# Raw first-layer weights in 128-partition transfers, queries ahead of keys, and another order of work in the first four chunks

## The chip, the core and the metric

The kernel runs on one core of a Trainium2 chip. The metric is device time in microseconds (us) of one execution; three executions before the change gave 628.51, 629.78 and 630.63, a median of 629.78 us. One execution was taken with the profiler: it took 630.29 us, and its span, from the first to the last profiled instruction, is 628.6 us. All times inside the profile count from the span's start.

## The reference, cut to what matters

A retention layer (linear attention with decay), followed by a two-layer feed-forward block whose activation is h * erf(softplus(h)):

```python
# q, k, v: (4 batches, 8 heads, 768 positions, 64), float32
for t in range(S):
    state = gamma[None, :, None, None] * state + np.einsum('bhd,bhe->bhde', k[:, :, t], v[:, :, t])
    y[:, :, t] = scale * np.einsum('bhd,bhde->bhe', q[:, :, t], state)
x = y.transpose(0, 2, 1, 3).reshape(B * S, H * D)     # 3072 tokens x 512
h = x @ w_in                                          # 512 x 2048
sp = np.maximum(h, 0.0) + np.log1p(np.exp(-np.abs(h)))
g = h * erf(sp)
return (g @ w_out).astype(np.float32)                 # 2048 x 512
```

Both weight matrices are 64-bit floats: `w_in` is 512 x 2048 x 8 bytes, 8.39 MB. The kernel gets them as 64-bit words and makes 32-bit floats of them itself.

## The kernel before, in words

**Tokens.** The 3072 tokens are 24 chunks of 128 (six for each batch). Two chunks make a group of 256 tokens, so there are twelve groups. Within a chunk the retention is two masked matrix products and a product with the running state.

**Weights.** `w_in` is handled in eight raw pieces, n = 0 to 7, each with 256 of the 2048 columns. One raw piece fills a tile `raw` of 128 partitions x 1024 64-bit words (1 MB). Partition p of its lower half (r = 0) holds rows of `w_in` below 256, the upper half (r = 1) those from 256 on, in four blocks g of 64 rows. `load_piece` issues the transfers, on SyncE's queue (SP, line 153). Each transfer before the change writes one half of the partitions: 64 partitions, two or four blocks g, and 128 or 256 columns. `conversion(n)` (lines 184 to 210) turns a raw piece into 32-bit floats: five passes of VectorE (DVE) with one of ScalarE (ACT, line 187) after the first. The pool has four raw tiles; the load of piece n+4 is issued when piece n is converted, and the loads of chunks 4 and 5 stand behind those of pieces 4 and 5.

**Stages.** (1) Four chunks of retention, written out by hand as a list of calls: `T` transposes keys (part 0) or queries (part 1) on TensorE (PE, line 390), `Q_` and `V_` scale queries and values on DVE (line 376), `S_` makes scores (line 402), `M` masks them (line 413), `O_` makes outputs (lines 434, 441, 449), `A` adds to the state (line 459). `keep_warm` puts idle products on PE (line 354). (2) A loop over sixteen column tiles `ft` of 128: `hidden_of(ft, g)` makes the first layer for groups 0 and 1 (line 591); tile ft needs piece ft // 2 converted, and the loop asks for tile ft + 2 ahead. Beside it run the retention of chunks 4 and 5, the loads of chunks 6 and 7 (32-partition transfers, line 123) and the splitting of the weights into high and low parts (lines 247 to 249). `put_hidden` stores each tile (256 KB) through GpSimd's queue (POOL, line 601). (3) Units: groups 2 to 11, eight units each, `unit(g, n)` with all weights on chip (lines 616 and 628), and beside them the rest of the retention and the conversion of `w_out`. (4) Activation and second layer (line 801).

**What sets the order.** Every engine runs its instructions in the order in which the program lists them; nothing reorders them. SP issues its transfers in program order and rotates through eight semaphores, so that a transfer is issued only when the one eight places before it has landed.

The lines that the change touches are `load` (103 to 106), `load_piece` (145 to 158), the opening loads (276 to 283), the guard in `ret_transpose` (393) and the list of calls of stage 1 (649 to 691). A piece is now loaded by

```python
rows = (slice(2), slice(2, 4)) if n == 0 else (slice(4),)
for part, g, r in itertools.product(parts or (None,), rows, range(2)):
```

Of the kernel before, what the change touches and what calls it, by code (L numbers as in the profile page):

```python
# [21 lines left out]
P = 128  # L22
C = 128
JPC = 4
# [17 lines left out]
def kernel(  # L42
# [14 lines left out]
    B, H, S, D = q.shape  # L57
# [5 lines left out]
    n_k = d_model // P  # L63
    n_ft = d_ff // P
    NPC = n_ft // 2
    DH = d_model // 2
# [13 lines left out]
    def b4(name, shape, dtype=F32):  # L80
        return big.tile([P] + shape, dtype, name=name, tag="b4")
# [4 lines left out]
    def b8(name, shape, dtype=F32):  # L86
        return wide.tile([P] + shape, dtype, name=name, tag="b8")
# [5 lines left out]
    KN, QN, V, KB, QB, KT, QT, SC, AM, SU = {}, {}, {}, {}, {}, {}, {}, {}, {}, {}  # L93
    KNP, VP = {}, {}

    def of_chunk(x, j):

        b, c = divmod(j, NC)
        return x[b, :, c * C : (c + 1) * C, :].rearrange("h p d -> p h d")

    def load(j):

        kq = b4("kq", [2, H, D])
        KN[j], QN[j] = kq[:, 0], kq[:, 1]
        for to, src in ((KN[j], k), (QN[j], q)):
            nc.sync.dma_start(to, of_chunk(src, j))  # L106

    def load_values(j):
        if j % 2 == 0:
            VP[j] = b4("v", [2, H, D])  # L110
        V[j] = VP[j - j % 2][:, j % 2]
        nc.sync.dma_start(V[j], of_chunk(v, j))
# [30 lines left out]
    WF, RAW, POWER = {}, {}, {}  # L143
    done = set()

    def load_piece(n, *parts):

        if n not in RAW:
            RAW[n] = b8("raw", [2 * d_model], I64)
        rows = (slice(2), slice(2, 4)) if n == 0 else (slice(4),)  # L150
        for part, g, r in itertools.product(parts or (None,), rows, range(2)):
            f = slice(2 * P) if part is None else slice(part * P, (part + 1) * P)
            nc.sync.dma_start(
                RAW[n][r * D : (r + 1) * D].rearrange("p (g f) -> p g f", g=n_k)[:, g, f],
                w_in[r * DH : (r + 1) * DH, n * 2 * P : (n + 1) * 2 * P].rearrange(
                    "(g p) f -> p g f", p=D
                )[:, g, f],
            )

    def load_quarter(i):  # L160
# [11 lines left out]
    def conversion(n):  # L172
# [5 lines left out]
        for part in range(2) if n < 4 else (None,):  # L178
# [22 lines left out]
            if part != 0:  # L201
                del RAW[n]
                if n + 4 < NPC:
                    load_piece(n + 4)
                if n < 2:
                    load(JPC + n)
                    load_values(JPC + n)
# [13 lines left out]
    def weights():  # L221


        for n in range(2 * NPC):
            yield from conversion(n)

    weight_steps = weights()
# [5 lines left out]
    def need(*what):  # L233
        while what not in done:
            next(weight_steps)
# [34 lines left out]
    nc.scalar.dma_start(d_k, decay_k)  # L270
    nc.scalar.dma_start(d_s, decay_s[::D].rearrange("(o s) h -> o s h", o=1).to_broadcast([P, 2, HP]))
    load(0)

    nc.scalar.copy(idle_out, ident[:, :1])

    for j in range(1, JPC):
        load(j)
        load_values(j - 1)
    load_piece(0, 0)
    load_values(JPC - 1)  # L280
    load_piece(0, 1)
    for n in range(1, 4):
        load_piece(n, 0, 1)

    causal = const.tile([P, C], F32, name="causal")
    nc.gpsimd.memset(causal, 1.0)
# [16 lines left out]
    def query_scale(c):  # L303
        nc.vector.reciprocal(kq_s[:, c, 1], kq_s[:, c, 0])
        nc.vector.tensor_scalar(kq_s[:, c, 1], kq_s[:, c, 1], unscale, None, op0=ALU.mult)
# [14 lines left out]
    def other_scales():  # L320
        query_scale(slice(2, NC))
# [30 lines left out]
    def keep_warm(n):  # L352
        for _ in range(n):
            nc.tensor.matmul(idle, ident, ident, start=True, stop=True)
# [3 lines left out]
    def ret_psum(pool=None):  # L358

        pool = pool or next(psum_turn)  # L360
        return pool.tile([P, HP, C], F32, name="hp" if pool is ps_h else "r")
# [3 lines left out]
    def x_of(j):  # L365

        g, i = divmod(j, 2)
        if i == 0:
            XC[g] = b4("xT", [HP, GT])
        return XC[g][:, :, i * C : (i + 1) * C]  # L370
# [13 lines left out]
    def ret_transpose(j, part=None, names=None):  # L384
        for i, (x, store) in enumerate(((KN[j], KT), (QN[j], QT))):
            if part not in (None, i):
                continue
            p = ps_o.tile([P, HP, C], F32, name=names[i]) if names else ret_psum(ps_h if i else ps_r)
            for u in range(HP):
                nc.tensor.transpose(  # L390
                    p[:, u, :], x[:, 2 * u : 2 * u + 2, :].rearrange("p h d -> p (h d)"), ident
                )
            if i == 0:
                KQT = b4("kqT", [2, HP, C])
                KT[j], QT[j] = KQT[:, 0], KQT[:, 1]
            nc.scalar.copy(store[j], p)
# [20 lines left out]
    def ret_out(j, between=None, state_last=False):  # L417
        c = j % NC
        x = x_of(j)
        pp = [ps_o.tile([P, HP, C], F32, name=f"o{(2 * j + r + 1) % 4}") for r in range(2)]  # L420

        def place(h):
            return pp[h % 2][h // 4 * D : (h // 4 + 1) * D, h % 4 // 2, :]

        if state_last:
            between()


        if c:
            for u in PAIRS:  # L430
                for r in range(2):
                    h = 2 * u + r
                    own = slice(r * D, (r + 1) * D)
                    nc.tensor.matmul(
                        place(h), state[own, u, :], QT[j][own, u, :],
                        start=(h % 4 < 2), stop=False, skip_group_check=True,
                    )
        if between is not None and not state_last:
            between()
        for h in (0, 4, 1, 5, 2, 6, 3, 7):  # L440
            nc.tensor.matmul(
                place(h), V[j][:, h, :], AM[j][:, h % 2, h // 2, :],
                start=(not c and h % 4 < 2), stop=True, skip_group_check=True,
            )

        new = SU[j] = pp[0][:, 2:, :].rearrange("p a (b d) -> p (a b) d", d=D)
        for h in range(H):
            r = h % 2
            nc.tensor.matmul(
                new[r * D : (r + 1) * D, h // 2, :], KN[j][:, h, :], V[j][:, h, :],  # L450
                start=False, stop=True, skip_group_check=True,
            )
        for r in range(2):
            nc.scalar.copy(x[:, r::2], pp[r][:, :2, :])
# [130 lines left out]
    def hidden_of(ft, g):  # L585

        if ft not in HP_:
            HP_[ft] = ps_h.tile([P, 2, GT], F32, name="hp")
        w = WF[ft // 2].rearrange("p h a f -> p (h a) f")
        for kk in range(n_k):  # L590
            nc.tensor.matmul(  # L591
                HP_[ft][:, g],
                w[:, kk, ft % 2 * P : (ft % 2 + 1) * P], XC[g][:, kk],
                start=(kk == 0), stop=(kk == n_k - 1),
            )
# [10 lines left out]
    def unit(g, n):  # L606
# [36 lines left out]

    Q_, V_, T, S_, M, O_, A = (
        scale_q, scale_v, ret_transpose, ret_scores, ret_mask, ret_out, ret_add
    )


    T(0, 0)
    keep_warm(2)  # L650
    Q_(0)
    second_scales()
    T(0, 1)
    keep_warm(1)
    T(1, 0)
    S_(0)
    Q_(1)
    T(1, 1)
    keep_warm(2)
    other_scales()  # L660
    M(0)
    V_(0)
    S_(1)
    Q_(2)
    O_(0)
    T(2, 0)
    M(1)
    A(0)
    T(2, 1)
    V_(1)  # L670
    Q_(3)

    def next_scores():
        S_(2)
        M(2)

    O_(1, next_scores)
    T(3, 0)
    V_(2)
    A(1)  # L680
    T(3, 1)
    need("in", 0)
    O_(2)
    S_(3)
    V_(3)
    next(weight_steps)
    A(2)
    M(3)
    need("in", 1)
    ret_out(JPC - 1, lambda: hidden_of(0, 0), state_last=True)  # L690
    hidden_of(1, 0)


# [217 lines left out]
    for n in range(NG * NU):  # L911
        g, i = divmod(n, NU)
# [62 lines left out]
```

## Time and profile before

| what | value |
|---|---|
| median of three executions | 629.78 us (628.51 to 630.63) |
| profiled execution | 630.29 us, of which span 628.6 us |
| PE busy | 617.5 us, 98% of the span |
| weight loads of PE | 555.9 us, 88% |
| DVE busy | 472.9 us, 75% |
| ACT busy | 346.8 us, 55% |
| POOL busy | 99.8 us, 16% |
| granted clock of TensorE | 0.999 |
| SP's transfers | 67.53 MB, 44.4% of sixteen DMA engines' span |
| POOL's transfers | 37.77 MB, 17.7% |
| raw pieces, 512 KB transfers | 8, median 10.3 us from issue to landing |
| raw pieces, 256 KB transfers | 12, median 6.2 us |
| raw pieces, 128 KB transfers | 8, median 5.5 us |

How to read it: the first rows are busy times of engines over the whole span and say little about a single stage. The change acts in the first 90 us, so the timelines of SP, DVE and PE in that stretch, and the table of the DMA engines' share and rate by stretch, are what to read. A DMA share of 1 means that the packets' times add up to all sixteen engines' time; since packets of one engine overlap a little, it can be above 1.

### The profile page before, as it was taken

To read this page: it belongs to the slowest core of one execution; us is meant where nothing else is said; L and a number is where in the kernel's file an instruction comes from. 1 tells how busy PE (TensorE), PEld (TensorE's weight loads), DVE (VectorE), ACT (ScalarE), POOL (GpSimd) and SP (SyncE) were. 2 spreads that over 40 slices of the span, in tenths; PEclk is the share of its full clock that TensorE was granted. 3 is DMA by queue.
4 is the path that set the end of the run, shared out by engine and by line. 5 is a ranking of instruction groups with operands and counts; after the bars stand their busy time and mean duration, and the time that the engine had idled before them with its cause. 6 is when DMAs were issued, how large, how long until landed. Compare 5 with 4: busy or idle time off the path is not lost.

```text
span 628.6 us, 14668 instructions
## 1 busy us (share of the span) xinstructions
PE 617.5 (98%) x6080; PEld 555.9 (88%) x6080; DVE 472.9 (75%) x608; ACT 346.8 (55%) x430; POOL 99.8 (16%) x189
## 2 busy tenths in 40 slices
PE   8899999999999999999999999999999999999997
PEld 7688789999999999999999978888888888888886
DVE  4887899849598887878777997867676686768650
ACT  3333353322323333232349779898889889888920
POOL 1054442222322413222111110000000000000000
PEclk9999999999999999999999999999999999999999
DMA  9999888986859898787945751453334314432300
GB/s 190 209 217 213 227 211 192 244 224 150 242 142 262 207 237 227 214 219 190 271 165 167 261 170 70 136 168 101 115 119 168 129 43 162 139 94 103 101 33 34
DMA packets 165426, 106.37 MB, mean 169 GB/s; under 512 B 139632, under 2 KB 143984, under 8 KB 165360
## 3 DMA queue, kind: packets, MB, share of 16 engines
q1 hardware_dynamic: 152608, 67.53, 44.4%
q0 software_dynamic: 12192, 37.77, 17.7%
q8 instruction: 47, 0.77, 0.5%
q10 hardware_dynamic: 560, 0.14, 0.1%
q14 instruction: 19, 0.16, 0.1%
HBM read 69.75 MB, written 35.65 MB: 168 GB/s over the span
## 4 chain that ended last, share of the span: by engine, by line
PE 89%; DMA 6%; SPq 2%; DVE 1%; issue 1%; POOL 1%; ACT 0%; DVEq 0%; POOLq 0%
PE o L616 35%; PE o L801 21%; PE hp L801 10%; PE r L801 10%; PE hp L591 4%; DMA hid<-h 3%; DMA kq_b<-decay_k_dram 2%; SPq L106 1%; DMA v<-in_v_dram 1%; PE hp L497 1%; PE hp L616 1%; PE r L616 1%; PE r L542 1%; DMA raw<-in_moe_w_in_dram 1%; PE hp L504 1%; PE r L553 1%
## 5 line engine op out<-in xcount | busy, mean ns | idle before, releaser
L616 PE MATMUL o<-x_hi,w_hi 128*128 128x256 f32 x600 | 149.6, 287 | 0.0
L616 PE MATMUL o<-x_lo,w_lo 128*128 128x256 f32 x600 | 147.2, 283 | 0.6 <-issue 0.6
L616 PEld LDWEIGHTS o<-x_hi,w_hi 128*128 128x128 f32 x600 | 115.0, 192 | 2.1 <-issue 0.7
L263 ACT ACTIVATE h<-o 128x512 f32<-128x512 f32 x75 | 44.7, 596 | 127.9 <-PE o L616 127.1
L616 PEld LDWEIGHTS o<-x_lo,w_lo 128*128 128x128 f32 x600 | 115.1, 192 | 0.1
L756 DVE TENSOR_TENSOR e<-hid,e 128x1024 f32<-128x1024 f32 x48 | 56.6, 1222 | 58.2 <-ACT e L746 58.2
L616 PE MATMUL o<-x_dif,w_dif 128*128 128x256 f32 x600 | 84.1, 283 | 0.0
L639 POOL DMA_DIRECT2D hid<-h x80 | 44.6, 558 | 206.7 <-DVE h L264 204.3
L616 PEld LDWEIGHTS o<-x_dif,w_dif 128*128 128x128 f32 x600 | 77.4, 192 | 0.0
L801 PE MATMUL o<-w_dif,g_dif 128*128 128x512 f32 x192 | 73.7, 389 | 0.0
L264 DVE SCALAR_TENSOR_TENSOR h<-o,h 128x512 f32<-128x512 f32 x75 | 51.2, 683 | 25.5 <-ACT h L263 13.1
L801 PE MATMUL o<-w_lo,g_lo 128*128 128x512 f32 x168 | 65.4, 389 | 0.0
L801 PE MATMUL o<-w_hi,g_hi 128*128 128x512 f32 x168 | 65.4, 389 | 0.0
L257 DVE SCALAR_TENSOR_TENSOR g_dif<-g_hi,g_lo 128x1024 fp32r<-128x1024 f32 x48 | 58.8, 1225 | 3.2
L255 ACT ACTIVATE g_hi<-e 128x1024 fp32r<-128x1024 f32 x48 | 51.0, 1063 | 17.8 <-DVE e L756 15.1
L256 DVE TENSOR_TENSOR g_lo<-e,g_hi 128x1024 fp32r<-128x1024 f32 x48 | 58.6, 1222 | 0.2
L591 PE MATMUL hp<-xT,w 128*128 128x256 f32 x256 | 56.9, 381 | 1.6 <-DVE w L210 1.6
L591 PEld LDWEIGHTS hp<-xT,w 128*128 128x128 f32 x256 | 48.1, 190 | 8.3 <-issue 1.2
L746 ACT ACTIVATE e<-e 128x1024 f32<-128x1024 f32 x48 | 48.2, 1053 | 0.3
L742 ACT ACTIVATE e<-hid 128x1024 f32<-128x1024 f32 x48 | 48.2, 1052 | 0.3
L801 PEld LDWEIGHTS o<-w_dif,g_dif 128*128 128x128 f32 x192 | 36.0, 188 | 7.5
L801 PE MATMUL hp<-w_dif,g_dif 128*128 128x512 f32 x96 | 37.5, 390 | 0.6 <-DVE h L264 0.6
(166 smaller groups left out, 1069.9 us busy)
## 6 DMA issues: line engine op xcount, KB each, us to landing
hid<-hid SPq DMA_DIRECT2D x48, 512.0 KB, 4.8
hid<-h POOLq DMA_DIRECT2D x80, 256.0 KB, 3.6
raw<-in_moe_w_out_dram POOLq DMA_DIRECT2D x32, 256.0 KB, 5.1
v<-in_v_dram SPq DMA_DIRECT2D x24, 256.0 KB, 5.7
out_dram<-y SPq DMA_DIRECT2D x23, 256.0 KB, 2.1
kb<-in_k_dram SPq DMA_DIRECT2D x144, 32.0 KB, 3.2
qb<-in_q_dram SPq DMA_DIRECT2D x144, 32.0 KB, 3.0
kn<-in_k_dram SPq DMA_DIRECT2D x18, 256.0 KB, 6.7
```

Of the source, the lines that this page charges most:

```text
L255: nc.scalar.activation(hi, x, AF.Copy, scale=KEEP)
L256: nc.vector.tensor_tensor(lo, x, hi.bitcast(F32), op=ALU.subtract)
L257: nc.vector.scalar_tensor_tensor(dif, hi.bitcast(F32), Z, lo.bitcast(F32), op0=ALU.mult, op1=ALU.subtract)
L263: nc.scalar.activation(to, a, AF.Copy, scale=1 + 1 / Z)
L264: nc.vector.scalar_tensor_tensor(to, b, -1 / Z, to, op0=ALU.mult, op1=ALU.add)
L591: nc.tensor.matmul(HP_[ft][:, g], w[:, kk, ft % 2 * P : (ft % 2 + 1) * P], XC[g][:, kk], start=(kk == 0), stop=(kk == n_k - 1),)
L616: nc.tensor.matmul(to[:, u], W[n][i][:, kk * 2 * P + u * P : kk * 2 * P + (u + 1) * P], X[g][i][:, kk], start=(u == 0 and kk == 0 and i == ...
L639: nc.gpsimd.dma_start(HID[g][:, 2 * n : 2 * n + 2], h)
L742: nc.scalar.activation(E[n], HID_[n], AF.Softplus)
L746: nc.scalar.activation(E[n], E[n], AF.Erf)
L756: nc.vector.tensor_tensor(E[n], HID_.pop(n), E[n], op=ALU.mult)
L801: nc.tensor.matmul(Y[g][t][x // 2], G[n][x][:, f, t * P : (t + 1) * P], W_OUT[ft // 2][x][:, ft % 2 * d_model : (ft % 2 + 1) * d_model], s ...
```

## The change

Three edits. `load_piece` takes one block g at a time for both halves of the partitions, so one transfer writes 128 partitions x 128 or 256 words; piece 0 is still loaded in two column parts of four transfers each, the other pieces in four transfers of 256 KB each. `load` issues queries ahead of keys, and the opening loads are put in another order (values of chunk 2 behind the first part of piece 0, values of chunk 3 behind the second). The list of calls of stage 1 transposes queries before keys, scores of a chunk come before the outputs of the chunk before, one `keep_warm` product is left out, and steps of the weights' conversion stand earlier in the list.

In the built program a raw transfer's destination counts, slowest first, 128 x 1 x 256 (128 x 1 x 128 for piece 0); its source counts 2 x 64 x 256 (2 x 64 x 128), because the two halves of the partitions come from rows 256 apart. Before, both sides counted 64 x 4 x 256, 64 x 4 x 128 or 64 x 2 x 128.

```diff
-        for to, src in ((KN[j], k), (QN[j], q)):
+        for to, src in ((QN[j], q), (KN[j], k)):
             nc.sync.dma_start(to, of_chunk(src, j))
...
-        rows = (slice(2), slice(2, 4)) if n == 0 else (slice(4),)
-        for part, g, r in itertools.product(parts or (None,), rows, range(2)):
+        for part, g in itertools.product(parts or (None,), range(n_k)):
             f = slice(2 * P) if part is None else slice(part * P, (part + 1) * P)
             nc.sync.dma_start(
-                RAW[n][r * D : (r + 1) * D].rearrange("p (g f) -> p g f", g=n_k)[:, g, f],
-                w_in[r * DH : (r + 1) * DH, n * 2 * P : (n + 1) * 2 * P].rearrange(
-                    "(g p) f -> p g f", p=D
-                )[:, g, f],
+                RAW[n].rearrange("p (g f) -> p g f", g=n_k)[:, g, f],
+                w_in[:, n * 2 * P : (n + 1) * 2 * P].rearrange("(r g p) f -> g r p f", r=2, p=D)[
+                    g, :, :, f
+                ],
             )
...
     for j in range(1, JPC):
         load(j)
-        load_values(j - 1)
+        if j < JPC - 1:
+            load_values(j - 1)
     load_piece(0, 0)
+    load_values(JPC - 2)
+    load_piece(0, 1)
     load_values(JPC - 1)
-    load_piece(0, 1)
     for n in range(1, 4):
-        load_piece(n, 0, 1)
+        load_piece(n)
...
-            if i == 0:
+            if j not in KT:
                 KQT = b4("kqT", [2, HP, C])
...
-    T(0, 0)
-    keep_warm(2)
     Q_(0)
     second_scales()
     T(0, 1)
-    keep_warm(1)
+    T(0, 0)
+    keep_warm(2)
+    Q_(1)
+    other_scales()
+    S_(0)
+    T(1, 1)
     T(1, 0)
-    S_(0)
-    Q_(1)
-    T(1, 1)
     keep_warm(2)
-    other_scales()
     M(0)
-    V_(0)
     S_(1)
     Q_(2)
+    V_(0)
+    T(2, 1)
+    T(2, 0)
     O_(0)
-    T(2, 0)
     M(1)
+    V_(1)
+    S_(2)
+    Q_(3)
     A(0)
-    T(2, 1)
-    V_(1)
-    Q_(3)
-
-    def next_scores():
-        S_(2)
-        M(2)
-
-    O_(1, next_scores)
-    T(3, 0)
+    M(2)
+    T(3, 1)
+    next(weight_steps)
+    O_(1, lambda: T(3, 0))
+    next(weight_steps)
     V_(2)
     A(1)
-    T(3, 1)
     need("in", 0)
+    S_(3)
     O_(2)
-    S_(3)
+    next(weight_steps)
+    M(3)
+    A(2)
     V_(3)
     next(weight_steps)
-    A(2)
-    M(3)
+    ret_out(JPC - 1, lambda: hidden_of(0, 0), state_last=True)
     need("in", 1)
-    ret_out(JPC - 1, lambda: hidden_of(0, 0), state_last=True)
     hidden_of(1, 0)
```

## The prediction

> **What bounds the kernel now.** I read the span's page first, then the timelines of SP, DVE and PE in the first 100 us, then the share and rate of the DMA engines by stretch.
>
> ```profile
> span 628.6 us, 14668 instructions
> PE 617.5 (98%) x6080; PEld 555.9 (88%) x6080; DVE 472.9 (75%) x608; ACT 346.8 (55%) x430; POOL 99.8 (16%) x189
> ```
>
> PE bounds the whole, so a change in the loads is worth only what PE waits for. On SP's timeline (start, duration, transfers issued) the raw weights follow the first chunks:
>
> ```profile
> 11.62 1.15 SPq L112 DMA_DIRECT2D v<-in_v_dram  x1
> 12.80 3.60 SPq L153 DMA_DIRECT2D raw<-in_moe_w_in_dram  x4
> 16.45 0.59 SPq L112 DMA_DIRECT2D v<-in_v_dram  x1
> 17.09 14.59 SPq L153 DMA_DIRECT2D raw<-in_moe_w_in_dram  x18
> 54.39 3.66 SPq L153 DMA_DIRECT2D raw<-in_moe_w_in_dram  x4
> ```
>
> The last raw piece is issued at 54 to 58 us and the loop over column tiles follows the weights closely. DVE's timeline shows where the last piece (n = 7) is converted, and PE's where the units begin:
>
> ```profile
> 77.81 0.73 DVE L184 TENSOR_SCALAR power<-raw 128x1024 uint32<-128x1024 uint32 x1
> 81.58 1.23 DVE L210 SCALAR_TENSOR_TENSOR w<-w,power 128x1024 f32<-128x1024 f32 x1
> 91.25 1.18 DVE L471 TENSOR_TENSOR qb<-qb,kq_b 128x1024 f32<-128x1024 f32 x1
> 97.01 0.68 DVE L264 SCALAR_TENSOR_TENSOR h<-o,h 128x512 f32<-128x512 f32 x1
> ...
> 90.72 0.47 PE L616 MATMUL o<-x_hi,w_hi 128*128 128x256 f32 x1
> 93.78 3.62 PE L628 MATMUL o<-xT,w 128*128 128x256 f32 x16
> 97.04 0.47 PE L616 MATMUL o<-x_hi,w_hi 128*128 128x256 f32 x1
> ```
>
> From 77.81 on DVE is idle 0.76 us until it puts the first unit away at 97.01, and PE starts its third unit, in the same PSUM tiles, at 97.04. So a later conversion of piece 7 moves everything behind it by as much. That conversion starts at 77.8 and is what I time.
>
> The table by stretch (columns: stretch, length with busy time and count for PE, PEld, DVE, ACT and POOL, granted clock, DMA share, GB/s) prices the transfers:
>
> ```profile
> 16.00:32.00 16.00, 12.97 (x176) 10.92 (x175) 13.10 (x26) 5.11 (x11) 0.00 (x0) 1.00 0.98 209
> 60.00:75.00 15.00, 13.88 (x169) 11.80 (x169) 12.54 (x17) 5.17 (x9) 4.61 (x9) 1.00 0.95 270
> 63.00:66.00 3.00, 1.88 (x33) 1.30 (x34) 1.28 (x4) 0.20 (x1) 1.46 (x3) 1.00 1.03 395
> 358.00:359.00 1.00, 1.00 (x10) 1.00 (x10) 1.00 (x2) 0.25 (x2) 0.29 (x1) 1.00 1.06 434
> ```
>
> With sixteen engines full, one engine moves 209/0.98/16 = 13.3 GB/s (half-partition raw transfers), 270/0.95/16 = 17.8, 395/16 = 24.7 (raw rows of 2 KB beside hidden stores) or 434/16 = 27.1 GB/s.
>
> **The raw transfers: how many engines carry one.** This decides. Every transfer of the kernel before has outermost counts of 32, 64 or 128, the same on both sides, so sixteen equal shares can be cut along the outermost count. The new raw transfers have 2 x 64 x 256 at the source against 128 x 1 x 256 at the destination. The largest cut that both outermost counts allow is 2. I take two engines, always the same two, as the work has to be cut somewhere and this is the only cut that needs no re-reading of the pattern. No row of the trace has such a form; the bounds are two engines and sixteen.
>
> The Trainium skill, page "DMA: Bandwidth & Descriptors", section "Why a DMA increments its semaphore by 16 and not by 1", states that the descriptor generator takes the largest number up to 16 that divides the slowest count above one of both sides, and the lowest-numbered engines for it. By that rule it is engines 0 and 1 here; no run so far shows it. The page's "Specifications" give about 27 GiB/s an engine; with that the raw bytes would take 145 us in place of my 170, an estimate, and the sum would be 732.
>
> **Their price.** 8.39 MB on two engines is 4.19 MB each. At 24.7 GB/s, the nearest row (2 KB raw packets with all partitions' ports in use), 170 us; at 27.1 GB/s 155 us; at 17.8 236 us; at 13.3 315 us. The same two engines carry a sixteenth of what else is due before the last raw byte: values of chunks 2 and 3, the three loads of chunks 4 and 5 (eight of 256 KB) and some 24 hidden stores of 128 KB, together 5.2 MB, 0.33 MB an engine: 13 us at 24.7, 25 us at 13.3; I take 19. The first raw transfer takes the eleventh place on SP, at 11.6 us in the row above; I add 2 us until bytes flow. The four raw tiles and eight semaphores keep at least four raw transfers in the queue, so the two engines do not run dry.
>
> The last raw piece lands at 11.6 + 2 + 170 + 19 = 202.6 us, and the first pass of its conversion, until now at 77.8, starts then: 124.8 us later. Queued behind that waiting pass on DVE are crossed sums, splits of x and weights and the first unit's put; PE's products of tiles 14 and 15 wait for its last pass, ACT's L187 for its first. The same happens at each piece before: a piece every 21 us (1 MB on two engines), against 6.9 us of PE for its two tiles.
>
> **What stands behind them on SP.** The loads of chunks 6 and 7 (16 of `kb`, 16 of `qb`) come after piece 7, and the eight semaphores let only eight of them out before it lands. The other 24 take 24/4 x 2.05 = 12.3 us by SP's rows from 70.42 to 78.57 (2.19, 1.93, 1.94, 1.93 for four, with small gaps), and 3.0 us to land: 15.3 us. DVE wants the last at 91.25 - 77.81 = 13.4 us. That adds 2 us, bounds 0 and 5.
>
> **PE after long waits.** PE's first fourteen products of the trace take 3.35 us, 0.24 each; later eight of the same kind take 1.04, 0.13. If PE is slow after waiting, the 16 products of tiles 14 and 15 cost 3.5 us more. PE reaches its third unit 5.1 + 3.5 + 2.9 + 3.5 = 15.0 us after the conversion begins, and DVE lets it go on at 19.2; so 4.2 us cover it: zero.
>
> **The edits with small prices.** Eight more raw issues (36 for 28) at a median of 0.61 us are 4.9 us of SP, which then waits for semaphores anyway. Queries ahead of keys swaps neighbours on SP, whose first two issues take 0.44 and 0.58 us. POOL's queue gets no new order. The list of calls of stage 1 keeps all its products but one `keep_warm` (two passes, 0.39 us), and moves scores, transposes and conversion steps by a few us within the first 30. All of this ends before piece 1 is there (about 57 us), so the raw weights hide it; without that cover it is rivals two and three.
>
> **The sum.** 628.6 + 124.8 + 2 = 755.4 us of span, and 1.7 us outside it as in the profiled execution (630.29 - 628.6): 757.1. That execution is 0.5 above the median of 629.78, which changes nothing here. Prediction 757.
>
> **Rivals.**
> One, two engines at a poor rate: 13.3 GB/s as at 16 to 32 us. Last landing at 11.6 + 2 + 315 + 25 = 353.6, time 628.6 + 275.8 + 3.7 = 908. For it: that stretch moved raw rows too. Against it: those packets were 1 KB, all sixteen engines wrote into 64 partitions, and 63 to 66 us shows 24.7 with more traffic, not less.
>
> Two, the other side: faster. The pieces go over sixteen engines and all partitions. Then the first stage's PE waits shrink: 1.41 us for the state before 19.97, 0.47 and 1.14 us for the weights before 23.68 and 29.10. If all 3.0 go, 630.29 - 3.0 = 627.3. It decides from eight engines on: eight at 24.7 carry 8.39 MB in 42 us, the last landing is then at 11.6 + 2 + 42 + 19 = 75, just under 77.8. For it: 209 GB/s at a share of 0.98 says that half-partition transfers are slow. The Trainium skill's "Rules for kernel authors" on the same page advise one 128-partition transfer over two halves. Against it: the source's outer count of 2.
>
> Three, sixteen engines, but the new order costs: values of chunk 3 are issued at about 19 instead of 16.45, four raw places later, and land 5.8 us on, at 24.8, where DVE scaled them at 23.45. That is 1.4 us late: 631.7.
>
> Four, another cut, say four engines: 85 us for the bytes, last landing 117.6, time 628.6 + 39.8 + 3.7 = 672.
>
> **How the numbers follow.** Chances: forecast 0.80, one 0.06, two 0.07, three 0.05, four 0.02. The forecast's own bounds: 27.1 GB/s, 13 us of other traffic and no wait for `qb` give a landing at 181.6 and 628.6 + 103.8 + 1.7 = 734; 17.8 GB/s with 25 us give 274.6 and 628.6 + 196.8 + 3.7 = 829. The range 734 to 829 holds the forecast and leaves out the rest, 0.2. What a measurement can tell from no change is 0.3%, 1.9 us. Faster: 0.05 of rival two. Same: 0.02 of two and 0.03 of three. Slower: 0.80 + 0.06 + 0.02 + 0.02 = 0.90.
>
> **What the changed profile would show.** Right: raw transfers of 256 KB landing tens of us after issue; a DMA share far under the 0.9s of before from 15 to 200 us at some 50 GB/s (two engines of sixteen is 0.13, the rest comes on top); DVE's L184 waiting for raw some 14 us at each piece; conversion 7 at about 203; PE's clock falling in the gaps; from the third unit on the same durations as before. Wrong: raw transfers landing in 5 to 10 us at 200 GB/s or more means sixteen engines; the same picture with a piece every 10 or 38 us means that the number of engines or their rate was off.

## The result

The changed kernel takes 755.99 us (median of six executions, 754.94 to 756.26) against 629.74 us of the kernel before: a ratio of 1.2005, 95% interval 1.1988 to 1.2022, 20% slower. The profiled execution took 754.94 us, its span is 752.9 us. The forecast was 757.

The page of the changed kernel: span, engines, and of the forty equal slices the granted clock and the DMA share (in tenths).

```profile
span 752.9 us, 14682 instructions
PE 637.2 (85%) x6078; PEld 569.7 (76%) x6078; DVE 473.1 (63%) x608; ACT 346.1 (46%) x430; POOL 98.8 (13%) x189
...
PEclk9777666866799999999999999999999999999999
DMA  8211222231378889789878855744334224443300
```

DVE's busy time stayed at 473 us; PE's rose by 20 us although its instructions did not, as the granted clock was down in slices two to eleven (19 to 207 us). All that was lost lies in these first 207 us.

The longest waits of DVE and of PE in the first 240 us (us in total, times, longest):

```profile
DVE power L183 <- DMA raw<-in_moe_w_in_dram: 114.8, 8, 17.2
PE hp L592 <- DVE w L209: 63.6, 5, 13.9
```

Two stretches of the table by stretch (start and end, length, busy us and instructions of PE, PEld, DVE, ACT and POOL, granted clock, DMA share, GB/s):

```profile
15.00:200.00 185.00, 82.94 (x648) 68.39 (x648) 50.74 (x85) 22.30 (x39) 24.49 (x46) 0.72 0.23 75
40.00:60.00 20.00, 10.28 (x72) 8.60 (x72) 4.07 (x8) 0.65 (x2) 0.00 (x0) 0.67 0.13 50
```

The first pass of a conversion waits 114.8 us in eight waits, 14.4 us each, for a raw piece. While nothing but raw pieces moves (40 to 60 us) the DMA share is 0.13, which is two of sixteen, and they carry 50 GB/s, 25 an engine.

The clearest view is that of the DMA engines from 8 to 26 us, in forty slices of 0.45 us: first queries, keys and values on all engines, then the raw transfers, then the values of chunk 2, then raw again.

```profile
DMA  9999999999999911111111111111159921111111
GB/s 216 222 216 217 218 216 220 217 217 217 217 219 218 184 46 48 46 46 46 46 46 48 43 48 46 46 46 46 46 143 236 244 68 46 46 46 46 46 46 38
```

SP's timeline shows the queue that this makes; the lines answer to those of before (the 22 raw transfers up to 31.7 us there):

```profile
11.43 6.20 SPq L152 DMA_DIRECT2D raw<-in_moe_w_in_dram  x4
17.67 2.74 SPq L112 DMA_DIRECT2D v<-in_v_dram  x1
20.46 9.70 SPq L152 DMA_DIRECT2D raw<-in_moe_w_in_dram  x4
32.99 80.91 SPq L152 DMA_DIRECT2D raw<-in_moe_w_in_dram  x16
153.56 32.47 SPq L152 DMA_DIRECT2D raw<-in_moe_w_in_dram  x8
```

The issue of a raw transfer itself became long. In the view of the tile `raw` (shortest/median/longest issue in ns, first and last start), before and then after the change:

```profile
L153 SPq DMA_DIRECT2D raw<-in_moe_w_in_dram x28: 595/614/2324, 12.8 to 57.1; - x28
```

```profile
L152 SPq DMA_DIRECT2D raw<-in_moe_w_in_dram x36: 692/3567/7917, 11.4 to 180.6; - x36
```

SP's waits for raw data to land sum to only 1.9 us in the first 205 us, so the eight semaphores are not what paced SP here. It was held in the issues. Still, several raw transfers are under way at a time: SP issues piece 1 from 32.99 us on, and DVE waits for the last of piece 0 until 38.77. If each took another pair of engines, the share would be above 0.13.

And the timelines of DVE and then of PE around the conversion of piece 7, which was at 77.81 before (start, duration, line, operation, and in brackets the wait ahead of it):

```profile
201.90 0.69 DVE L183 TENSOR_SCALAR power<-raw 128x1024 uint32<-128x1024 uint32 x1 [14.84 <-DMA raw<-in_moe_w_in_dram]
217.32 1.23 DVE L472 TENSOR_TENSOR qb<-qb,kq_b 128x1024 f32<-128x1024 f32 x1 [1.96 <-DMA qb<-in_q_dram]
223.12 0.68 DVE L263 SCALAR_TENSOR_TENSOR h<-o,h 128x512 f32<-128x512 f32 x1
```

```profile
207.00 8.88 PE L592 MATMUL hp<-xT,w 128*128 128x256 f32 x32 [11.57 <-DVE w L209]
215.53 0.47 PE L617 MATMUL o<-x_hi,w_hi 128*128 128x256 f32 x1
221.85 0.47 PE L617 MATMUL o<-x_hi,w_hi 128*128 128x256 f32 x1
223.95 1.12 PE L617 MATMUL o<-x_dif,w_dif 128*128 128x256 f32 x8
```

The conversion starts 124.1 us later. From it to the end of the span it is 551.0 us, before 550.8: everything behind it only moved.

### The profile page after: what moved, and what is told of

Read it like the earlier page. It is cut to its first block, busy times and chain, and to the rows that moved or that the text cites. A ratio compares the mean times of both kernels' runs of the same rounds, so it can differ in the third digit from the quotient of the medians.

```text
span 752.9 us, 14682 instructions
## 1 busy us (share of the span) xinstructions
PE 637.2 (85%) x6078; PEld 569.7 (76%) x6078; DVE 473.1 (63%) x608; ACT 346.1 (46%) x430; POOL 98.8 (13%) x189
## 4 chain that ended last, share of the span: by engine, by line
PE 72%; SPq 24%; DMA 3%; DVE 1%; issue 1%; DVEq 0%
PE o L617 29%; SPq L152 18%; PE o L800 17%; PE hp L800 9%; PE r L800 9%; SPq L106 4%; DMA raw<-in_moe_w_in_dram 3%; SPq L112 2%; PE hp L592 1%; PE hp L498 1%; PE hp L617 1%; PE r L617 1%; PE r L543 1%; PE hp L505 1%; PE r L554 1%; PE hp L543 1%
## 5 line engine op out<-in xcount | busy, mean ns | idle before, releaser
L592 PE MATMUL hp<-xT,w 128*128 128x256 f32 x256 | 71.0, 442 | 63.6 <-DVE w L209 63.6
L592 PEld LDWEIGHTS hp<-xT,w 128*128 128x128 f32 x256 | 57.0, 228 | 75.5 <-issue 65.4
L183 DVE TENSOR_SCALAR power<-raw 128x1024 uint32<-128x1024 uint32 (+1 forms) x20 | 11.8, 588 | 114.8 <-DMA raw<-in_moe_w_in_dram 114.8
L186 ACT ACTIVATE power<-power,below 128x512 uint32<-128x512 uint32 (+1 forms) x12 | 10.4, 864 | 144.6 <-DVE power L183 144.6
```

The lines of the kernel that those rows point to most:

```text
L592: nc.tensor.matmul(HP_[ft][:, g], w[:, kk, ft % 2 * P : (ft % 2 + 1) * P], XC[g][:, kk], start=(kk == 0), stop=(kk == n_k - 1),)
```

## The experiments

Theory: a transfer is cut along the outermost count that both sides allow, so the raw transfers run on two DMA engines, always the same two. Rivals: the new order of work costs the time; transfers that write all partitions are slow in themselves; any mismatch of the two patterns is slow; the limit is one of SP's queue. Times of before beside them are 628.94 to 629.35 us in the median. Where no ratio is given beside a time, it is that of one execution.

### The raw edit alone, and everything but the raw edit

The kernel before with the new `load_piece` and one transfer per block (`load_piece(n)` for n = 1 to 3):

```diff
+                w_in[:, n * 2 * P : (n + 1) * 2 * P].rearrange("(r g p) f -> g r p f", r=2, p=D)[
+                    g, :, :, f
+                ],
```

> The kernel before with the raw transfers of the change alone (2 x 64 at the source), its queries, keys and order of work left as they were. Two engines: the last raw piece still lands after 8.39 MB on two engines, so 752 to 760 us. Rival, the new order of the first chunks costs the time: about 630 us, as before. Rival, both share it: something between, 660 to 720 us.

Measured: 755.82 us. The last conversion starts as in the changed kernel:

```profile
202.00 0.69 DVE L183 TENSOR_SCALAR power<-raw 128x1024 uint32<-128x1024 uint32 x1 [14.79 <-DMA raw<-in_moe_w_in_dram]
```

The changed kernel with the transfers of before:

```diff
+        rows = (slice(2), slice(2, 4)) if n == 0 else (slice(4),)
+        for part, g, r in itertools.product(parts or (None,), rows, range(2)):
...
+                RAW[n][r * D : (r + 1) * D].rearrange("p (g f) -> p g f", g=n_k)[:, g, f],
```

> The changed kernel with the raw transfers of before (one half of the partitions each, 64 at the outermost on both sides); queries ahead of keys and the new order of work stay. Two engines: all of the loss is gone, 627 to 632 us, and what is left of a difference to before is the worth of the other edits, between 3.0 us gained (the three waits of PE for weights and state in the first 30 us) and 1.4 us lost (values of chunk 3 later). Rival, the order costs the time: about 756 us.

Measured: 627.05 us, ratio 0.9971 (0.9951 to 0.9992). The raw edit makes all of the loss; the rest of the change gains 0.3%, just clear of nothing. The rival of the order is out.

### The outermost count: 128, 4, 8, 16

Only the source's rows change; bytes, destinations and the number of transfers (36) stay.

```diff
-                w_in[:, n * 2 * P : (n + 1) * 2 * P].rearrange("(r g p) f -> g r p f", r=2, p=D)[
+                w_in[:, n * 2 * P : (n + 1) * 2 * P].rearrange("(r g p) f -> g r p f", r=4, p=P // 4)[
```

and likewise r = 8 and r = 16; for 128 the pattern is `"(g p) f -> g p f"` with p = 128.

> The changed kernel, but each raw transfer takes 128 consecutive rows of w_in, so that both sides count 128 at the outermost; same bytes, same destinations, same number of transfers. Partition p of block g then holds row 128 g + p, so other rows of w_in are paired with x than the reference pairs: another product is computed. Two engines: with 128 on both sides all sixteen engines carry a transfer, so 626 to 632 us, and DMA shares near 0.9 with more than 209 GB/s while raw pieces load. Rival, a transfer that writes all 128 partitions is slow in itself (36 instead of 28 transfers, 2 KB rows, ports): still 740 to 760 us.

> The changed kernel with four at the source's outermost (4 x 32 rows for 128 partitions) instead of two; same bytes and destinations. Block g of partition quarter r holds rows 128 r + 32 g on, so other rows of w_in are paired with x: another product is computed. Cut along the outermost count, four engines: 85 us for the raw bytes, 19 for the rest, last landing near 118 us, time 668 to 680 us, raw loading near 100 GB/s. Rival, any source pattern that doesn't match the destination runs on two engines or on one: 750 us or more. Rival, sixteen engines as soon as the counts are not two: about 630 us.

> The changed kernel with eight at the source's outermost (8 x 16 rows); same bytes and destinations. Block g of partition eighth r holds rows 64 r + 16 g on, so other rows of w_in are paired with x: another product is computed. Cut along the outermost count, eight engines: 42 us for the raw bytes, last landing near 75 us, which the prediction took as the point from which the load is hidden: 626 to 633 us, and raw loading alone near 200 GB/s. Rival, the loss follows from a mismatch of the two patterns and not from the count: above 660 us.

> The changed kernel with sixteen at the source's outermost (16 x 8 rows); same bytes and destinations. Block g of partition sixteenth r holds rows 32 r + 8 g on, so other rows of w_in are paired with x: another product is computed. In e5 eight engines moved 160 GB/s while raw bytes went alone, 20 an engine, where two moved 24.9 and four 24.6 each. If that comes from the cut by blocks of neighbouring partitions, sixteen such blocks move 16 x 20 = 320 GB/s or fewer; if eight was a matter of the bytes' addresses, 380 GB/s and more as in e3. Either way the weights are early: 626 to 629 us. Rival to the count as the cause: above 632 us.

| outermost count at the source | time, us | conversion of piece 7 starts | rate with raw alone | GB/s per engine |
|---|---|---|---|---|
| 2 (the change) | 755.99 | 201.90 | 50 GB/s, share 0.13 (40 to 60 us) | 25 |
| 4 | 671.66 | 118.86 | 100 GB/s, share 0.26 (36 to 40 us) | 25 |
| 8 | 633.81 | 81.72 | 160 GB/s, share 0.53 (24 to 29 us) | 20 |
| 16 | 627.37 | 72.14 | 283 GB/s, share 1.07 (25 to 30 us) | 17.7 |
| 128 | 626.60, ratio 0.9946 (0.9927 to 0.9964) | 72.09 | 395 GB/s, share 1.05 (25 to 30 us) | 24.7 |

The first column's effect in the DMA view, first of count 4 from 36 to 46 us, then of count 8 from 20 to 40 us:

```profile
DMA  2222222222222222222222222227849333232333
GB/s 98 98 98 98 98 106 106 98 98 98 98 98 98 98 106 98 98 98 98 106 90 107 98 98 98 98 98 279 311 164 393 131 100 102 108 100 98 100 115 100
```

```profile
DMA  9655675555555555555555555555557875565645
GB/s 247 144 156 181 147 188 194 160 156 160 164 160 160 156 160 164 160 160 156 164 160 164 152 160 160 164 160 156 164 164 221 266 250 150 156 189 148 169 156 205
```

The share follows the count: 2, 4, 8 and 16 sixteenths. (The destination counted 128 throughout; a small count on its side was not tried.) The rival that writing all partitions is slow is out (128), and so is that of any mismatch (4, 8 and 16 mismatch too). Count 4 came at 671.66, where the rival of another cut had 672. Count 8 missed its band by 0.8 us: its engines moved 160 GB/s and not 198, so the raw bytes took 52 us in place of 42, and piece 7 was converted at 81.72, later than before the change. Counts 4, 16 and 128 came out inside their bands. Sixteen mismatched blocks move less than 128 matching rows do, by the table of the same stretch, in which only raw pieces move, 16 before 128:

```profile
25.00:30.00 5.00, 4.99 (x62) 4.38 (x59) 4.30 (x9) 1.37 (x3) 0.00 (x0) 1.00 1.07 283
```

```profile
25.00:30.00 5.00, 5.00 (x62) 4.38 (x55) 4.30 (x9) 1.37 (x3) 0.00 (x0) 1.00 1.05 395
```

All sixteen are at work in both, so the number of engines is not the whole of it. The 283 GB/s lie on the side of a cut by blocks of neighbouring partitions (320 or fewer), but the two patterns also read other rows of `w_in`; which partitions an engine writes was not varied by itself, and the cause stays open.

### Another queue for half of the pieces

```diff
-            nc.sync.dma_start(
+            (nc.sync if n < 4 else nc.scalar).dma_start(
```

> The changed kernel (2 x 64 at the source) with raw pieces 4 to 7 issued from ACT's queue instead of SP's. Both queues use the same two engines for such a transfer: nothing is gained, 750 to 775 us (ACT may lose some time waiting to issue). Rival, the limit of 50 GB/s is one of the queue, or each queue has two engines of its own: half of the bytes go beside the other half, last landing near 118 us, 665 to 700 us.

Measured: 763.51 us. Where raw transfers of both queues are under way (88 to 96 us; SP's queue is q1, ACT's q10), the queues move the same (MB, share of sixteen engines), together 50 GB/s:

```profile
q1 hardware_dynamic: 97, 0.20, 6.7%
q10 hardware_dynamic: 97, 0.20, 6.4%
```

The two shares add up to two engines of sixteen: the queues take turns on one pair. ACT's first four issues lasted from 82 to 120 us, and in this time no engine computed:

```profile
82.00:120.00 38.00, 0.00 (x0) 0.00 (x0) 0.00 (x0) 0.00 (x0) 0.00 (x0) 0.50 0.21 67
```

(The share of 0.21 holds loads of chunks 4 and 5, too.) So a second queue brings no second pair, and the run is 7.5 us longer than the change; ACT's long issues, behind which its computing stands, are the likely reason.

The same with `nc.gpsimd` for pieces 4 to 7:

> The changed kernel (2 x 64 at the source) with raw pieces 4 to 7 issued from POOL's queue. If POOL's descriptors also go to two engines, but to another pair from transfer to transfer, the pieces 4 to 7 no longer wait behind 0 to 3 on one pair: piece 7 is issued when piece 3 is converted, near 110 us, and its conversion starts near 125 to 135 us: 675 to 690 us. If it is the same pair as for SP: 750 to 765 us. The Trainium skill, page DMA: Bandwidth & Descriptors, section Why a DMA increments its semaphore by 16 and not by 1, states the former for POOL's queue; no run so far shows it.

Measured: 705.01 us, outside both bands, but far from that of one pair. The stretch after POOL issued piece 4, of this kernel and then of the changed one:

```profile
43.00:58.00 15.00, 6.97 (x46) 5.88 (x44) 1.21 (x3) 0.65 (x2) 3.36 (x4) 0.84 0.34 102
```

```profile
43.00:58.00 15.00, 8.06 (x48) 6.71 (x44) 1.11 (x2) 0.65 (x2) 0.00 (x0) 0.73 0.13 50
```

102 GB/s at a share of 0.34 is more than one pair gives, so POOL's transfers use other engines, too. They are not free for SP: its pieces 1, 2 and 3 are converted at 66.6, 89.8 and 119.2 us, against 60.7, 83.4 and 105.6 in the changed kernel, and conversion 7 starts at 150.5 (125 to 135 expected). From 46 to 58 us SP's queue moved 0.32 MB:

```profile
q1 hardware_dynamic: 158, 0.32, 7.2%
```

At 50 GB/s it would be 0.60. What is missing is about one transfer of 0.26 MB, as if one of POOL's four had gone to SP's pair; the profile does not name engines, so that is an argument and not shown.

### The small edits

> The kernel of e2 (half-partition transfers, new order of calls and of opening loads) with keys loaded ahead of queries again. If the 2.3 us that e2 gained come from the order of calls, 626.5 to 627.5 us; if they need the queries first, since the new order scales and transposes queries first, 628 to 630 us.

> The kernel before with queries loaded ahead of keys and nothing else. Its first call transposes keys of chunk 0, which land about 1 us later, then scales queries: no gain by itself, 629 to 631 us. If the queries' place alone made the gain of e2: 627 us.

The edits are the line of `load`, turned back in the kernel of e2 and put alone into the kernel before. Measured: 628.36 us, ratio 0.9988 (0.9972 to 1.0004), and 628.65 us, ratio 0.9994 (0.9979 to 1.0009). Neither alone is told from no change. The first time lies in the band of the second reading, that the order needs the queries first; the second is 0.35 us below the band of no gain. The traces say a little more. The long run of first-layer products that follows chunk 3 starts before the change at (all four lines up to 32 us)

```profile
29.10 3.26 PE L591 MATMUL hp<-xT,w 128*128 128x256 f32 x14 [1.14 <-DVE w L210]
```

and in e2 (the halves with the new order), e10 (the order alone) and e11 (the queries' place alone) at

```profile
27.55 4.77 PE L593 MATMUL hp<-xT,w 128*128 128x256 f32 x21
```

```profile
27.96 4.34 PE L593 MATMUL hp<-xT,w 128*128 128x256 f32 x19
```

```profile
28.60 3.69 PE L591 MATMUL hp<-xT,w 128*128 128x256 f32 x16 [0.57 <-DVE w L210]
```

that is 1.55, 1.14 and 0.50 us earlier: the order brings most of it there. The conversion of piece 7 says the same, at 77.81 before and at 73.32, 73.72 and 77.65 in these three. The traces so point to the order and the times to the two together; each trace is one execution, and how the 0.3% is shared stays open.

A last try to go below e2, with piece 0 ahead of queries and keys of chunk 3:

```diff
+        if j == JPC - 1:
+            load_piece(0, 0)
         load(j)
...
+    A(0)
+    M(2)
+    O_(1)
+    next(weight_steps)
     Q_(3)
-    A(0)
-    M(2)
     T(3, 1)
-    next(weight_steps)
-    O_(1, lambda: T(3, 0))
+    T(3, 0)
+    A(1)
     next(weight_steps)
     V_(2)
-    A(1)
```

> The kernel of e2 (half-partition transfers, the new order) with the first part of piece 0 issued ahead of queries and keys of chunk 3, and the first conversion step placed behind the outputs of chunk 1, queries of chunk 3 scaled and transposed after it. In e2 DVE waited 2.23 us for that part at 18.57 and PE 2.0 us for a copy of ACT queued behind the conversion's activation. Theory: the conversion of piece 0 is what the first stage ends on, so 1 to 2 us fewer than e2: 625 to 626.5 us. Rival, DVE is full from there on and the wait only moves to the queries of chunk 3: 626.5 to 628.5 us, no difference.

Measured: 626.73 us, ratio 0.9968 (0.9951 to 0.9985), no different from e2, as the rival said; the 625 to 626.5 us of the theory were missed. DVE's wait for the raw piece is gone, but conversion 7 starts at 73.37 instead of 73.32: the wait went elsewhere before the conversions end. e2 and e8 are both faster than the kernel before, by 0.3%.

## Why the prediction was right

**How many engines carry a transfer** was the step that decided, and it held: share 0.13 with raw alone, and the loss goes with the outermost count from 2 over 4 and 8 to 16. The rule of the Trainium skill ("DMA: Bandwidth & Descriptors", section "Why a DMA increments its semaphore by 16 and not by 1") agrees with these runs at every count that was tried, also in that SP's and ACT's queues share a pair and POOL's goes to further engines. Which numbers the engines have, no view shows.

**Their price**: the row of 63 to 66 us was the right one to take. The two engines moved 46 GB/s in piece 0 (1 KB rows) and 50 after it: 1.05 MB / 46 + 7.34 MB / 50 is 170 us, as taken. From the first issue at 11.4 to 201.9 leaves 20.5 us, where 2 + 19 stood for start and other traffic. That this agrees is in part luck. The reason given for a queue that never runs dry did not hold: not the eight semaphores but the long issues paced SP. The loads of queries and keys of chunks 4 and 5, which stand between pieces 4, 5 and 6, took SP 5.0 to 5.7 us each. Behind them the first two issues of pieces 5 and 6 took 0.76 to 0.87 us again, as into a queue with little left, and the rate was 36 GB/s for a moment (near 128 and 154 us). What this cost of the 20.5 us was not measured. The 27 GiB/s an engine of the Trainium skill ("DMA: Bandwidth & Descriptors", section "Specifications") were not reached; the sum by this figure, 732, would have been 24 us short.

**The shift** of everything behind conversion 7 is 124.1 us (124.8 forecast), but my reason for it was only half right. PE's third unit does not wait for DVE's put: it starts at 221.85, the put at 223.12. Only the unit's last eight products, which go into its second PSUM tile, the one that DVE reads, need the put; they start at 223.95, just after it, and PE does not wait.

**PE after long waits** was mis-sized. Tiles 14 and 15 are 32 records, 6.9 us, not 16 and 3.5; in the gaps' clock they took 8.5 us (207.00 to 215.53). PE's own chain from the conversion to the third unit was 5.1 + 8.5 + 6.3 = 19.95 us, against 19.23 before, not 15.0. There was no cover of 4.2 us, and the term was not zero: the slow clock cost up to 1.6 us, of which some 0.9 came back because PE began these tiles right after the conversion and not, as before, about 1 us later. That the shift still fits is luck: half of the records left out and a wait that did not exist cancelled.

**What stands behind them on SP**: DVE did wait 1.96 us for `qb`, as forecast (2). It held up no product there, since PE needs the put only 2.1 us into its unit. So the 2 us of the sum were not paid: what both terms leave at the end is the 0.2 us between 551.0 and 550.8.

**The sum** by terms of the profiled execution: 628.6 + 124.1 + 0.2 + 2.0 outside the span is 754.9; forecast 628.6 + 124.8 + 2 + 1.7.

**The edits with small prices** are hidden as said: e1 without them is at 755.82. Uncovered, in e2, they gain 0.3% and do not lose; rival three's late values of chunk 3 did not show as a loss.

**Rival two's point of decision**, eight engines, was set a little low, since eight moved 160 GB/s and not 198. Its time for sixteen, 627.3, is what counts 16 and 128 gave (627.37 and 626.60), but not for its reason: e2 has 627.05 with the transfers of before. The median of count 128 is 0.45 us below that of e2, and their intervals overlap, so what faster raw transfers add to the new order is not told from nothing.

**What the profile would show**: the waits of 14 us and the fallen clock were there. Landing times for SP's transfers were not: the page gives none in this kernel, so the waits had to serve.

## What to carry to other kernels

Look at the built counts of both sides of a transfer, slowest first, before believing its number of partitions: "writes 128 partitions" said nothing here, "2 at the source" everything, and the DMA share in a stretch where one kind of transfer runs alone tells the number of engines. The length of the issues is a second sign. When two halves of a tile come from far apart, two transfers with 64 in front beat one with 2 in front by four times in rate. And a transfer that is hidden with room to spare can become the bound of a whole stage by one rearrange.

## What had not been expected of the hardware

Fewer, larger cuts are not all alike. With raw pieces alone, two and four engines moved 25 GB/s each, and sixteen engines with 128 matching rows 24.7 each; but eight blocks of 16 partitions moved 20 each and sixteen blocks of 8 partitions 17.7. Transfers on two engines also held SP and ACT where these issued them: 3.57 us for an issue of SP in the median, against 0.61 before, and 38 us for four of ACT, while issues of POOL took 0.82 us in the median. Transfers from ACT with the same pattern shared SP's pair; those from POOL did not all do so.
